# The third burst of k^T v one q group earlier, and a small first transfer from W_qkv

## The chip, the cores and the metric

The kernel runs on one core of a Trainium2 chip. The time is the device time of one execution in microseconds (us), as the median of several runs. TensorE (PE) multiplies matrices and has its own queue of weight loads (PEld); VectorE (DVE), ScalarE (ACT) and GpSimd (POOL) work on tiles; SyncE (SP) issues most transfers. Every engine runs its own instructions in order, and engines wait for each other through semaphores. Beside the queues that move data, the trace has queues of the kind "instruction": packets that bring the engines' programs.

## The reference, cut to what matters

The sizes are S = 2048 tokens, D = 640, 32 heads of 20, and F = 1536. All inputs are bf16.

```python
h  = x + A(_layernorm(x), A_wqkv, A_w_phi, A_wo)
h2 = h + B(_layernorm(h), B_w_gate, B_w_up, B_w_down)

def A(x, wqkv, w_phi, wo):          # linear attention
    q, k, v = split_heads(x @ wqkv)
    pq, pk  = q @ w_phi, k @ w_phi  # per head, 20 x 20
    phi_q = concat(softmax(pq), softmax(-pq))
    phi_k = concat(softmax(pk), softmax(-pk))
    kv, z = phi_k^T @ v, sum over tokens of phi_k
    return merge_heads((phi_q @ kv) / (phi_q @ z + 1e-6)) @ wo

def B(x, w_gate, w_up, w_down):
    return (gelu(x @ w_gate) * (x @ w_up)) @ w_down
```

## The kernel before

The 2048 tokens are 16 tiles of 128, in four groups `b` of four. The order of the instructions of TensorE and SyncE is written out by hand; what the other engines do is written in the same order.

At the start SyncE issues the tiles of x (`x_sb`) and the v part of W_qkv (`Wv`, in three pieces, lines 194 to 197), and ScalarE issues `wphi` (line 191) and loads its table of functions (line 192). TensorE runs 30 matmuls on ones (`warm`, line 230), then transposes the first two tiles of x (`tr_c`) and computes the v of tiles 0 and 1 from the first pieces of `Wv` (`v_part`, line 312). `BD` (line 433), which VectorE builds from `wphi`, is needed by `fold`, which multiplies W_phi into the k and q parts of W_qkv (`Wk2`, `Wq2`).

The loop of line 494 goes over the 16 token tiles `t`. `k_tile(t)` multiplies the normalised tile by `Wk2` (10 matmuls) and ScalarE exponentiates it with both signs into `Ek[t]` (line 340). `k_norm(t)` sums each head on VectorE (line 347), takes the reciprocal (line 351) and multiplies it into `Ek[t]` (line 355): the second sign on GpSimd always, the first on GpSimd for the tiles of `VP` (9, 11, 12 and 13 among them), on VectorE for the others.

`kv_tile(t)` (line 374) adds phi_k^T v of tile t into one PSUM tile `kvp`: 32 heads, each one weight load of 32 columns and one matmul over 40 columns. So a tile is 32 pairs of very short instructions. They are not run tile by tile but in bursts: tiles 0 to 3 at t = 9 and tiles 4 to 8 at t = 13 (`KVG`), tiles 9 to 12 at t = 15 (`KVQ`, the third burst), and tiles 13 to 15 after the loop (line 540).

At t = 15 the loop of line 508 also computes the first four of the 13 q groups. `q_mm(j)` (line 396) has 10 matmuls over 512 columns for a group of two, 5 for a group of one; `q_exp(j)` (line 401) exponentiates the group on ScalarE with both signs. `QG` lists the groups: group 0 reads the token group b = 1, group 1 reads b = 0. `KVQ` says behind which q group the third burst stands:

```python
for j in range(len(QT)):
    if t == QT[j]:
        q_mm(j)
        q_exp(j)
        for i in KVQ.get(j, ()):
            kv_tile(i)
```

At t = 13 SyncE is given the load of `Wo` (800 KB, line 534), and after the loop those of `Wg` (line 538), `Wu` (line 554) and `Wd` (line 559). The `Wg` load is held back by a small copy on GpSimd (line 536) that reads the exponentials of q group 2. After `kv_mask` the kernel runs the rest of the q groups mixed with the attention of the first tiles (`attn_a` and so on), and then the feed-forward part (`gate_up`, `down`) with the attention of later tiles woven in.

Of the kernel before, what the change touches and what calls it, by code (L numbers as in the profile page):

```python
# [8 lines left out]
BF16 = mybir.dt.bfloat16  # L9
# [8 lines left out]
def kernel(  # L18
# [12 lines left out]
    nc = tc.nc  # L31
    P = 128
    S = 2048
    D = 640
# [19 lines left out]
    T3 = 3  # L54

    KVG = {9: (0, 1, 2, 3), 13: (4, 5, 6, 7, 8)}
    KVQ = {1: (9, 10, 11, 12)}
    VC = Dh + 1
    KC = Dh + 2

# [17 lines left out]
    const = ctx.enter_context(tc.tile_pool(name="const", bufs=1))  # L78
# [20 lines left out]
    BD = const.tile([P, NC, 8, Dh], BF16, name="BD")  # L99
    nhalf = const.tile([P, 2], F32, name="nhalf")  # L100
    eps = const.tile([P, 1], F32, name="eps")

    def eq(t, c, s):
        for E, g in zip(Eq, QG):
            if t // 4 * NC + c in g:
                return E[:, g.index(t // 4 * NC + c), s, t % 4 * P:(t % 4 + 1) * P]
# [81 lines left out]
    nc.gpsimd.memset(eps, EPS)  # L188
    nc.sync.dma_start(x_sb[0][:, 0:1, :], x_v[:, 0:1, :])
    nc.sync.dma_start(x_sb[0][:, 1:2, :], x_v[:, 1:2, :])  # L190
    nc.scalar.dma_start(wphi, phi_v.rearrange("(c p) f -> p c f", p=P))
    nc.scalar.add_instruction(mybir.InstLoadActFuncSet(name=nc.get_next_instruction_name(), act_func_set_id=6))
    nc.sync.dma_start(x_sb[0][:, 2:3, :], x_v[:, 2:3, :])  # L193
# [174 lines left out]
    def kv_tile(t):  # L368

        E = Ek[t].rearrange("p s (h f) -> p s h f", f=Dh)  # L370
        for i in range(QH):
            for r in range(4):
                h = r * QH + i
                nc.tensor.matmul(kvp[QUAD[r], :, i * Dh:(i + 1) * Dh], lhsT=vF[t % NV][:, h * VC:h * VC + 32],  # L374
                                 rhs=E[:, :, h, :], start=(i == t == 0), stop=(t == NT - 1), skip_group_check=True)
# [23 lines left out]
    def q_exp(j, signs=(0, 1)):  # L399
        for s in signs:  # L400
            nc.scalar.activation(Eq[j][:, :, s, :], pqs[j][:, 0:len(QG[j])], ACTF.Exp, scale=(1.0, -1.0)[s])  # L401
# [92 lines left out]
    for t in range(NT):  # L494
# [13 lines left out]
# [6 lines that stand above are left out]
# [423 lines left out]
```

## Time and profile before

| | |
|---|---|
| median of 3 runs | 271.94 us (271.78 to 272.07) |
| the profiled execution | 272.4 us |
| its span, first to last instruction | 270.7 us |
| PE busy | 265.7 us, 98% of the span, 2867 matmuls and 2867 weight loads |
| DVE / ACT / POOL busy | 174.9 / 138.9 / 101.2 us |
| granted TensorE clock, mean | 0.999 |
| instruction packets of queue q8 | 22, together 0.36 MB |

The profile is of one execution. Its page gives busy time by engine, the chain of work that ended last, the costliest groups of instructions, and the transfers. The trace behind it answers by time: the chain in order of time, all instructions of a stretch, the transfers of a stretch by queue, or the busy time and the granted clock of each engine in a stretch. "issue" in a row means that the engine was idle and the trace shows no wait that ended then. A matmul's end is modelled, its start is not.

### The profile page before, as it was taken

Reading aid. Unit: us, or ns where it says so; the run is one execution under the profiler, and the core shown is the slowest. Engines: PE = TensorE matmul, PEld = TensorE weight load, DVE = VectorE, ACT = ScalarE, POOL = GpSimd, SP = SyncE. Lnnn points to the kernel's source line nnn. Section 1 sums busy time; section 2 is a strip of 40 time slices with the busy share of each in tenths; the row PEclk is TensorE's granted clock in tenths of the full one; section 3 lists DMA queues with packets and bytes.
Section 4 is the critical chain, followed back from the end, with each engine's and each line's share of the span. In section 5 each row is a group of like instructions: output and inputs, shape, how many; then the busy total and the mean of one; then the engine's idle time right before and its main releaser. Section 6 shows DMA issues by size and latency. Waiting matters only on the chain.

```text
span 270.7 us, 7046 instructions
## 1 busy us (share of the span) xinstructions
PE 265.7 (98%) x2867; PEld 171.3 (63%) x2867; DVE 174.9 (65%) x347; ACT 138.9 (51%) x249; POOL 101.2 (37%) x238
## 2 busy tenths in 40 slices
PE   7999999999999999999999999999999999999995
PEld 6777777755455877788755455775555476444574
DVE  5889999996877767876466783568673332333322
ACT  5789998876789675245541356421544300322100
POOL 5548988796002335376211564014661100000000
PEclk9999999999999999999999999999999999999999
DMA  6998257250678432442201222102222101000011
GB/s 187 225 199 169 54 99 110 38 150 2 234 246 244 155 101 56 41 104 51 52 24 51 48 50 51 48 3 75 77 44 52 24 24 51 24 0 0 4 48 48
DMA packets 45264, 22.10 MB, mean 82 GB/s; under 512 B 37808, under 2 KB 43184, under 8 KB 45232
## 3 DMA queue, kind: packets, MB, share of 16 engines
q1 hardware_dynamic: 44576, 21.64, 32.6%
q8 instruction: 22, 0.36, 0.6%
q10 hardware_dynamic: 656, 0.03, 0.2%
q14 instruction: 10, 0.08, 0.1%
HBM read 10.18 MB, written 2.62 MB: 47 GB/s over the span
## 4 chain that ended last, share of the span: by engine, by line
PE 96%; DMA 2%; SPq 0%; issue 0%; DVE 0%
PE gu L767 39%; PE pd L789 19%; PE pq L396 8%; PE pk L296 8%; PE po L707 8%; PE pv L296 7%; PE kvp L374 2%; PE pv L312 2%; DMA Wv<-in_A_wqkv_dram 2%; PE ab L618 1%; PE wa L248 1%; PE ab L585 1%; PE tp L164 0%; SPq L193 0%; SPq L190 0%
## 5 line engine op out<-in xcount | busy, mean ns | idle before, releaser
L770 ACT ACTIVATE g<-gu 128x512 bf16<-128x512 f32 (+1 forms) x60 | 30.4, 510 | 73.8 <-PE gu L767 72.9
L773 DVE TENSOR_TENSOR GT<-gu,g 128x512 bf16<-128x512 f32 (+1 forms) x60 | 34.4, 580 | 46.7 <-PE gu L767 38.8
L767 PE MATMUL gu<-LN2T,Wg 128*128 128x512 bf16 (+1 forms) x300 | 61.8, 337 | 0.0
L767 PE MATMUL gu<-LN2T,Wu 128*128 128x512 bf16 (+1 forms) x300 | 61.7, 336 | 0.0
L789 PE MATMUL pd<-Wd,GT 128*128 128x320 bf16 (+4 forms) x396 | 53.9, 295 | 0.0
L789 PEld LDWEIGHTS <-GT 128*128 128x128 bf16 x396 | 37.6, 98 | 14.5 <-DVE GT L773 0.2
L767 PEld LDWEIGHTS <-Wu 128*128 128x128 bf16 x300 | 29.4, 98 | 22.6
L767 PEld LDWEIGHTS <-Wg 128*128 128x128 bf16 x300 | 29.0, 98 | 21.2
L296 PEld LDWEIGHTS <-LN1T 128*128 128x128 bf16 x290 | 27.9, 98 | 10.5
L355 POOL TENSOR_TENSOR E<-E,rs 128x640 bf16<-128x640 bf16 x25 | 31.6, 1299 | 4.4 <-DVE rs L351 4.1
L791 DVE TENSOR_TENSOR y<-pd,x_sb 128x320 bf16<-128x320 f32 (+4 forms) x33 | 15.8, 480 | 24.2 <-PE pd L789 24.2
L707 PE MATMUL po<-Wo,oT 128*128 128x320 bf16 x160 | 24.5, 299 | 0.0
L296 PE MATMUL pk<-Wk,LN1T 128*128 128x320 bf16 x160 | 24.4, 299 | 0.0
L396 PE MATMUL pq<-LN1T,Wq 128*128 128x512 bf16 x100 | 22.9, 379 | 0.0
L347 DVE TENSOR_REDUCE sk<-E 128x64 f32<-128x1280 bf16 x16 | 22.9, 1430 | 0.0
L401 ACT ACTIVATE Eq<-pq 128x1024 bf16<-128x1024 f32 (+1 forms) x26 | 19.9, 831 | 3.5 <-PE pq L396 3.3
L340 ACT ACTIVATE E<-pk 128x640 bf16<-128x640 f32 x28 | 18.7, 746 | 3.0 <-PE pk L296 3.0
L707 PEld LDWEIGHTS <-oT 128*128 128x128 bf16 x160 | 15.6, 98 | 7.3 <-ACT oT L165 0.2
L296 PE MATMUL pv<-Wv,LN1T 128*128 128x320 bf16 x130 | 19.8, 299 | 0.0
L151 ACT ACTIVATE ln<-x_sb,v,rstd 128x640 bf16<-128x640 bf16 x14 | 12.9, 920 | 13.4 <-POOL v L746 13.2
L396 PEld LDWEIGHTS <-Wq 128*128 128x128 bf16 x100 | 9.4, 98 | 10.3
L682 DVE TENSOR_TENSOR tt<-AB,w 128x1280 bf16<-128x1280 f32 x10 | 15.1, 1506 | 0.4 <-POOL w L675 0.3
(120 smaller groups left out, 290.6 us busy)
## 6 DMA issues: line engine op xcount, KB each, us to landing
out_dram<-y SPq DMA_DIRECT2D x15, 160.0 KB, 1.8
x_sb<-in_A_x_dram SPq DMA_DIRECT2D x6, 320.0 KB, 4.0
Wu<-in_B_w_up_dram SPq DMA_DIRECT2D x1, 1920.0 KB, 8.9
Wg<-in_B_w_gate_dram SPq DMA_DIRECT2D x2, 768.0 KB, 5.8
Wd<-in_B_w_down_dram SPq DMA_DIRECT2D x1, 1440.0 KB
Wo<-in_A_wo_dram SPq DMA_DIRECT2D x1, 800.0 KB, 5.2
x_sb<-in_A_x_dram SPq DMA_DIRECT2D x4, 160.0 KB, 3.3
Wv<-in_A_wqkv_dram SPq DMA_DIRECT2D x2, 320.0 KB, 4.2
```

Source lines behind the costliest of these rows:

```text
L296: nc.tensor.matmul(ps[:, u, 0:HD], lhsT=lnT(t, c), rhs=W[:, c, u * HD:(u + 1) * HD], start=(c == 0), stop=(c == NC - 1))
L340: nc.scalar.activation(Ek[t][:, s, :].rearrange("p (u f) -> p u f", u=2), pk[:, :, 0:HD], ACTF.Exp, scale=((lnp[t][2], nrstd[t]) if t in C ...
L347: nc.vector.reduce_sum(sk, Ek[t].rearrange("p s (h f) -> p (s h) f", f=Dh), axis=AX.X)
L355: eng.tensor_tensor(e, e, rs[:, s * H:(s + 1) * H, None].to_broadcast([P, H, Dh]), ALU.mult)
L396: nc.tensor.matmul(pqs[j][:, i, :], lhsT=Wq2[:, kc, c * P:(c + 1) * P], rhs=LN1T[b][:, kc, :], start=(kc == 0), stop=(kc == NC - 1))
L401: nc.scalar.activation(Eq[j][:, :, s, :], pqs[j][:, 0:len(QG[j])], ACTF.Exp, scale=(1.0, -1.0)[s])
L707: nc.tensor.matmul(pos[u], lhsT=st[t][:, c, :], rhs=Wo[:, c, u * HD:(u + 1) * HD], start=(c == 0), stop=(c == NC - 1))
L767: nc.tensor.matmul(gu[i][:, 0:n], lhsT=W[:, c, f * P:(f + 1) * P], rhs=LN2T[b][:, c, a0:a1], start=(c == 0), stop=(c == NC - 1))
L770: nc.scalar.activation(g[:, 0:n], gu[0][:, 0:n], ACTF.Gelu_apprx_tanh)
L773: nc.vector.tensor_tensor(st[b, "g", f][:, a0:a1], gu[1][:, 0:n], g[:, 0:n], ALU.mult)
L789: nc.tensor.matmul(pd[:, 0:f1 - f0], lhsT=st[b, "g", f][:, tl * P:(tl + 1) * P], rhs=Wd[:, f, f0:f1], start=(f == 0), stop=(f == NF - 1), ...
L791: nc.vector.tensor_tensor(y[:, f0:f1], pd[:, 0:f1 - f0], x_sb[b][:, tl, f0:f1], ALU.add)
```

## The change

The third burst, `kv_tile` of tiles 9 to 12, moves from behind q group 1 to behind q group 0. And a new transfer is put first in ScalarE's queue, ahead of `wphi`: 16 bf16 values (32 bytes) of every fifth row of W_qkv, from the first columns of the v part, into a tile `ahead` that nothing reads. It has 128 pieces, one for each partition, and touches rows 0, 5, 10 and so on to 635. Every other instruction stays as it was, and the counts of TensorE's instructions too.

```diff
@@ -54,7 +54,7 @@
     KVG = {9: (0, 1, 2, 3), 13: (4, 5, 6, 7, 8)}
-    KVQ = {1: (9, 10, 11, 12)}
+    KVQ = {0: (9, 10, 11, 12)}
@@ -99,6 +99,7 @@
     eps = const.tile([P, 1], F32, name="eps")
+    ahead = const.tile([P, 16], BF16, name="ahead")
@@ -188,6 +189,7 @@
     nc.sync.dma_start(x_sb[0][:, 0:1, :], x_v[:, 0:1, :])
     nc.sync.dma_start(x_sb[0][:, 1:2, :], x_v[:, 1:2, :])
+    nc.scalar.dma_start(ahead, A_wqkv.rearrange("(p r) n -> p r n", p=P)[:, 0, 2 * D:2 * D + 16])
     nc.scalar.dma_start(wphi, phi_v.rearrange("(c p) f -> p c f", p=P))
```

## The prediction

> **What bounds the kernel now.** I read the page's busy table first, then the chain of work that ended last, then the chain in order of time around the moved burst, then the transfers of that stretch, and last the first 7 us.
>
> ```profile
> PE 265.7 (98%) x2867; PEld 171.3 (63%) x2867; DVE 174.9 (65%) x347; ACT 138.9 (51%) x249; POOL 101.2 (37%) x238
> PE 96%; DMA 2%; SPq 0%; issue 0%; DVE 0%
> q8 instruction: 22, 0.36, 0.6%
> ```
>
> TensorE is busy for 98% of the span and makes 96% of the chain. After 6.45 us its chain has one hole before the end. So whatever delays or saves TensorE time in the middle reaches the end nearly in full. The chain in order of time (start, length, what) has that hole inside the third burst:
>
> ```profile
> 57.20 4.32 PE pq L396 x20
> 61.52 0.97 PE kvp L374 x109
> 62.50 0.48 issue
> 62.98 0.30 PE kvp L374 x19
> 63.28 3.34 PE pq L396 x15
> 66.62 0.87 PE kvp L374 x96
> ```
>
> The burst stops after 109 of its 128 pairs, in the middle of tile 12, before an instruction that carries no wait; the hole is 0.48 us and "issue" names no releaser. I take it for a lack of instructions. The queue q8 moves 22 packets of 16 KB, and TensorE has 2 x 2867 = 5734 instructions: one packet for 261 of them, near 256 of 64 bytes. A burst uses them at two in 8.9 ns (0.97 us / 109). The transfers in two neighbouring stretches, first 56.1 to 60.6 us, then 60.6 to 62.9 us:
>
> ```profile
> DMA packets 1306, 0.97 MB, mean 215 GB/s; under 512 B 677, under 2 KB 1306, under 8 KB 1306
> q1 hardware_dynamic: 1306, 0.97, 80.2%
> Wo<-in_A_wo_dram SPq DMA_DIRECT2D x1, 800.0 KB, 5.2
> ...
> q8 instruction: 1, 0.02, 2.8%
> q1 hardware_dynamic: 17, 0.01, 1.8%
> ```
>
> In the first stretch only data moves: a transpose, then `Wo`, issued at 56.17 us. In the second comes one instruction packet, which by the trace starts at 60.64 us, as the last packet of `Wo` ends (60.69 us), and takes 1.04 us, to 61.68 us. TensorE goes on at 62.98 us, 1.30 us later. The next packet starts at 64.10 us, 1.12 us after it went on, as if entering a block asks for the one after it. The packet at 72.59 us likewise starts only when the load of `Wg` ends (72.69 us). So I read: a block is asked for when the one before it is entered, it stands in line behind the data already queued, and is usable 1.3 us after it lands.
>
> **Part 1, the burst.** Nothing is added or removed: 128 pairs change places with 10 matmuls of q group 1. What counts is where the block border falls. TensorE's instructions are equal in number, so the border is the same instruction number in both orders. Before the hole stand 20 instructions of group 0, 21 of group 1 (one is a wait) and 218 of the burst, 259; the block of 256 thus begins with the fourth instruction of group 0. With the burst directly behind group 0, the 256 are 17 of group 0 and 239 of the burst: the border comes after 119 pairs, with 9 left.
>
> Times in the new order: group 0 begins at 57.20 us as before and takes half of 4.32, 2.16 us, to 59.36 us. The burst's data is there: the eight GpSimd products from 54.45 to 64.90 us are two each for tiles 11, 12 and 13 and one each for 14 and 15, 1.27 us each, so that tile 12's second, the fourth, ends at 59.40 us, while the burst comes to tile 12 only 96 x 8.9 ns = 0.85 us after 59.36. Tiles 9 to 11 are done by 57 us. The border is reached at 59.36 + 119 x 8.9 ns = 60.42 us. The block's packet depends on `Wo`, which SyncE issues behind transposes of work that stands ahead of group 0, so nothing before 59.36 us changes, and it is usable at 62.98 us again. The hole becomes 62.98 - 60.42 = 2.56 us. Then come 9 pairs (0.14 us, from 0.30 for 19) to 63.12 us and group 1, 2.16 us, to 65.28 us. In the trace of before, group 2 starts at 63.28 us: 2.00 us earlier. The change in short lets TensorE stand idle while group 1, which used to run in that time, is still to do.
>
> Is any of it given back? Behind the burst TensorE has no idle time that could take it up: the chain is TensorE without a hole to 267.83 us. Nor is more lost: group 3 needs the PSUM tile of group 0, whose exponentials end at 61.34 us as before. The exponentials of group 1 (1.94 us) run from 65.3 to 67.3 us, before group 2 ends at 67.44 us, so those of group 2, the copy on POOL that releases `Wg` on SP's queue, and everything behind them shift by the same 2.0 us. The next block's packet was asked for on entering this one, at 62.98 us, and is usable at 64.10 + 0.93 + 1.30 = 66.3 us as before; its border, near 67.3 us, comes at 69.3 us. No hole there. Cost of part 1: +2.00 us.
>
> The idle time itself is a risk for the clock. The nearest row is the end of the kernel: busy time by engine (us, with the count of instructions), granted clock, share of DMA and GB/s in three stretches.
>
> ```profile
> 262.00:266.90 4.90, 4.90 (x42) 3.76 (x41) 1.48 (x3) 0.00 (x0) 0.00 (x0) 1.00 0.19 67
> 266.90:270.30 3.40, 0.92 (x16) 0.74 (x13) 0.65 (x2) 0.00 (x0) 0.00 (x0) 1.00 0.18 48
> 270.30:270.70 0.40, 0.00 (x0) 0.00 (x0) 0.00 (x0) 0.00 (x0) 0.00 (x0) 0.52 0.00 0
> ```
>
> There the clock fell to about half after 3.4 us with 0.92 us of work. 3.4 us around the new hole would hold at least 0.84 us of work, and mostly more, as the hole would have to lie wholly in one such stretch.
>
> **Part 2, the transfer.** ScalarE issues it in about the 0.47 us that `wphi`'s issue takes at 0.79 us; `wphi` and the table load (1.28 us, ending at 2.56) move back by 0.47 us. Cover: ScalarE waits for x until 4.09 us, 1.06 us after the new end of the table load; `wphi` lands 2.9 us after its issue, so near 4.2 us, and is first read at 6.64 us. With those covers gone each would cost up to 0.47 us. On the 16 DMA engines, shared with x and `Wv`, 128 packets of 32 bytes cost what `wphi`'s 640 of 40 bytes do each, 11 ns: 0.09 us an engine.
>
> The first matmuls on `Wv` show what could be gained:
>
> ```profile
> 2.18 4.22 DMA Wv<-in_A_wqkv_dram
> 5.46 1.29 ACT L165 COPY LN1T<-tp 128x640 bf16<-128x640 bf16 x2
> 6.20 0.10 PEld L312 LDWEIGHTS <-LN1T 128*128 128x128 bf16 x1 [0.30 <-ACT LN1T L165]
> 6.45 1.79 PE L312 MATMUL pv<-Wv,LN1T 128*128 128x320 bf16 x12 [0.37 <-DMA Wv<-in_A_wqkv_dram]
> 2.00:3.50 1.50, 1.50 (x17) 1.50 (x16) 0.54 (x6) 0.57 (x1) 1.23 (x9) 1.00 0.98 240
> 3.50:4.50 1.00, 1.00 (x13) 0.86 (x10) 0.95 (x3) 0.41 (x1) 0.65 (x13) 1.00 0.75 119
> 4.50:7.00 2.50, 1.71 (x20) 1.28 (x20) 2.14 (x6) 2.33 (x7) 0.52 (x2) 1.00 0.98 336
> ```
>
> Around 3.5 to 4.5 us, when the queue comes to `Wv`, the rate dips to 119 GB/s between 240 and 336, with packets of up to 0.98 us in the trace: some 0.6 us lost, and perhaps a first touch of W_qkv's memory, which the new transfer would take earlier. Even so TensorE can't start on `Wv` before its weights, loaded from 6.20 us: gain at most 6.45 - 6.26 = 0.19 us. The other end: the same 0.6 us is lost in front of x's first tile instead, whose landing (VectorE starts on it at 3.36 us) leads to that weight load; 6.26 + 0.6 is 0.4 us later than now. The row nearest is the wait of 0.37 us on `Wv` itself, so I take a small gain, -0.1 us, and keep -0.2 and +0.4.
>
> **Sum.** +2.00 - 0.10 = +1.9 us. The profiled execution took 272.4 us, 1.7 around its span of 270.7 us, and lies 0.5 us above the median of the runs, 271.94. Its own forecast is 274.3; that of the median, which I give, 273.8 us, 0.7% slower.
>
> **Rivals.** (a) The packet gets through while `Wo` moves. It must start by 60.42 - 1.30 - 1.04 = 58.1 us, and then the hole is gone, old and new: 271.94 - 0.48 - 0.1 = 271.4 us, faster. Each us later costs one, up to the 2.56. For it: block and request stand there from about 57.3 us on. Against it: with the old order the same request waited until 60.64. The Trainium skill, "DMA: Bandwidth & Descriptors" (Queues, rings and completion order), says that each DMA engine goes round-robin between the queues that have work, which would favour this rival; the starts at 60.64 and 72.59 us, each as the data ended, disagree. "Runtime: NRT & Kernel Launch" (Instruction fetch mechanics) of the same skill even gives TensorE room for 2048 instructions and calls the fetch mostly hidden; a hole of 0.48 us with no wait at a 256-instruction border speaks against it here.
> (b) The hole has nothing to do with a block and goes with the burst, 0.48 us wherever it stands: 271.94 - 0.1 = 271.8 us, no change.
> (c) The clock halves for one stretch of 3.4 us after the hole, which loses 1.7 us: 275.5 us. For it the row at 266.9 us; against it that 0.84 us is the least and not the usual work of such a stretch. The skill's "TensorE: Matmul & The Clock Gate" (Part 1: The HAM clock gate) asks for about one idle window of 3.4 us, and by that rule nothing would be lost.
>
> **How the numbers follow.** Forecast, hole of about 2.6 us: 0.66, itself 273.3 to 274.4 by the bounds of part 2 and some 0.3 us for where the border falls. (c) 0.11. (a) 0.10 and a packet partly ahead, between 271.6 and 273.3, 0.06. (b) 0.07. From 272.8 to 275.6 lie the forecast, (c) and some of the partial case, about 0.8. What a measurement of this kernel can tell from no change is about 0.2%, 0.54 us. Faster: (a) less a little, 0.10; same: (b) and a little, 0.09; slower: 0.81.
>
> **What would show it.** In the chain, an "issue" row of 2.3 to 2.8 us inside the third burst, behind about 119 pairs, ending near 63 us; an instruction packet that starts with the end of `Wo`; group 2 starting near 65.2 us; the first matmul on `Wv` between 6.2 and 6.9 us; granted clock at 1.00 from 62 to 70 us. A hole ending early, or none, proves the reading of the packet queue wrong; a start on `Wv` outside those bounds, part 2.

## The result, and the profile after

The changed kernel takes 273.39 us (median of 8 runs, 272.26 to 277.14), the kernel before 271.98 us (271.78 to 272.87, 8 runs). The ratio is 1.0046, with a 95% interval of 1.0029 to 1.0063: slower by about half a per cent, where 0.7% was forecast. All ratios here leave out runs of over 1.5% above the fastest of the same kernel (here one, 277.14 us); medians and ranges keep them. The profiled execution took 273.48 us, with a span of 271.8 us. But its trace is not the one that was forecast.

The busy table and the chain that ended last, from the page of the changed kernel:

```profile
PE 265.3 (98%) x2867; PEld 170.9 (63%) x2867; DVE 175.1 (64%) x347; ACT 138.9 (51%) x249; POOL 100.5 (37%) x238
PE 93%; DMA 3%; DVE 1%; SPq 0%; issue 0%
```

TensorE still bounds the kernel, with transfers for 3% of the chain instead of 2%. The chain in order of time (start, length, what), first at the start, then around the burst, then where a new wait has come in:

```profile
2.18 5.00 DMA Wv<-in_A_wqkv_dram
7.22 1.79 PE pv L314 x12
...
58.09 2.16 PE pq L398 x10
60.24 1.13 PE kvp L376 x128
61.38 5.50 PE pq L398 x25
...
83.19 4.20 DMA LN2T<-ln
87.39 0.14 issue
87.52 3.44 PE gu L769 x30
```

The first matmul on `Wv` starts at 7.22 us, 0.77 later than before (6.45). The burst runs through in 1.13 us without any hole. And at 87.4 us TensorE waits for a transposed tile, which it did not before. The waits of TensorE (in us: total, times, longest) say the same:

```profile
PE pv L314 <- DMA Wv<-in_A_wqkv_dram: 1.5, 1, 1.5
PE gu L769 <- DMA LN2T<-ln: 0.9, 1, 0.9
```

Where the 1.1 us of span went, by the starts of the same work in both traces: +0.77 at the first matmul on `Wv` (7.22 against 6.45) and +0.89 at q group 0 (58.09 against 57.20); +0.26 at group 2 (61.38 + 2.16 = 63.54 against 63.28), so the burst without its hole gave back 0.63; +1.22 at the first matmul of `gate_up` (87.52 against 86.30), most of it the 0.9 us wait. That wait is for a transpose behind the load of `Wu`, which took 10.1 us from issue to landing in this execution and 8.9 before.

The transfers from 56.1 to 60.6 us, the stretch that held only data before:

```profile
q1 hardware_dynamic: 1097, 0.71, 61.8%
q8 instruction: 1, 0.02, 2.1%
Wo<-in_A_wo_dram SPq DMA_DIRECT2D x1, 800.0 KB, 5.8
```

The instruction packet is now inside it. By the trace it starts at 58.23 us, when the first packet of `Wo` starts (58.24), and not when the last one ends.

### The profile page after: what moved, and what is told of

Read it like the earlier page. It is cut to its first block, busy times and chain, and to the rows that moved or that the text cites. A ratio compares the mean times of both kernels' runs of the same rounds, so it can differ in the third digit from the quotient of the medians.

```text
span 271.8 us, 7047 instructions
## 1 busy us (share of the span) xinstructions
PE 265.3 (98%) x2867; PEld 170.9 (63%) x2867; DVE 175.1 (64%) x347; ACT 138.9 (51%) x249; POOL 100.5 (37%) x238
## 4 chain that ended last, share of the span: by engine, by line
PE 93%; DMA 3%; DVE 1%; SPq 0%; issue 0%
PE gu L769 38%; PE pd L791 19%; PE pk L298 8%; PE po L709 8%; PE pv L298 7%; PE pq L398 6%; DMA Wv<-in_A_wqkv_dram 2%; PE kvp L376 2%; PE pv L314 2%; DMA LN2T<-ln 2%; PE ab L620 1%; PE wa L250 1%; PE ab L587 1%; DVE x_sb L718 1%; DVE stats L122 1%; PE tp L165 0%
## 5 line engine op out<-in xcount | busy, mean ns | idle before, releaser
L122 DVE BATCH_NORM_STATS2 stats<-x_sb 128x6 f32<-128x320 bf16 x32 | 13.9, 475 | 2.0 <-DMA x_sb<-in_A_x_dram 2.0
## 6 DMA issues: line engine op xcount, KB each, us to landing
Wu<-in_B_w_up_dram SPq DMA_DIRECT2D x1, 1920.0 KB, 10.1
```

The lines of the kernel that those rows point to most:

```text
L122: nc.vector.bn_stats(stats[:, j, i, :], xt[:, i * HD:(i + 1) * HD])
```

## The experiments

Each ratio is against the kernel before, run beside it on the same chip. "Hole" is TensorE's idle time at the block border, of the one profiled execution. The theories are: (A) the hole is the wait for an instruction packet that races with `Wo`'s data; (B) it goes with the burst for some other reason; and for the transfer (C) and (D), where its cost comes from.

### The burst alone

```diff
-    KVQ = {1: (9, 10, 11, 12)}
+    KVQ = {0: (9, 10, 11, 12)}
```

> The burst behind group 0, without the new transfer. Theory A (a block of 256 TensorE instructions is fetched when the one before it is entered, and the fetch queues behind Wo's data if it comes second): the request and Wo's first packet come within some 0.3 us of each other, so single runs fall on two values: no hole, 272.0 - 0.5 = 271.5 us, or a hole of 2.0 to 2.6 us, 273.5 to 274.0 us. Theory B (the 0.48 us hole goes with the burst and has no block behind it): 272.0 us in all runs, hole 0.48 us.

Measured: 272.99 us (12 runs, 272.08 to 277.17) against 272.12; 1.0045 (1.0016 to 1.0074). Seven runs lie between 272.08 and 273.09, five between 274.38 and 277.17, none between. The profiled one, 272.61 us, is of the first group:

```profile
59.73 1.06 PE kvp L374 x119
60.79 0.33 issue
61.12 0.23 PE kvp L374 x9
...
61.73 5.13 PE pq L396 x23
```

The hole stands behind 119 pairs with 9 left, exactly where the block border was worked out, but is 0.33 us long. The packet starts at 57.67 us, just ahead of `Wo`'s first (57.77), and takes 1.97 us, while `Wo`'s packets move. Two groups of runs speak for (A), though the upper one lies above the 273.5 to 274.0 us expected. The lower group was expected 0.5 us under the kernel before; by its median (272.57) it is 0.45 us above, which these runs do not explain.

The same kernel once more:

> The kernel with the burst behind group 0 alone once more, for a second profile and a few more times. Theory A (race of the packet with Wo's data): the profile shows one of two pictures, the packet starting before or with Wo's first data and a hole under 0.4 us, or the packet starting with the end of Wo's data and a hole of 2.0 to 2.6 us; single times near 272.5 us or over 274.3 us, and few between.

Measured: 276.97 and 278.15 us; 1.020 (1.017 to 1.023, two runs only). This profile holds the other picture. The chain in order of time:

```profile
59.82 1.06 PE kvp L374 x119
60.88 2.93 issue
63.81 0.23 PE kvp L374 x9
64.04 0.32 PE pq L396
64.36 0.14 issue
64.50 6.73 PE pq L396 x23
```

The transfers of the same execution, first 56.1 to 60.6 us, then 60.6 to 62.9 us:

```profile
q1 hardware_dynamic: 1201, 0.84, 69.0%
...
q1 hardware_dynamic: 127, 0.14, 17.0%
q8 instruction: 1, 0.02, 2.6%
```

Again 119 pairs, then 2.93 us of nothing, somewhat more than the 2.0 to 2.6 expected. The packet starts at 61.45 us, when `Wo`'s data ends (61.44), and lands at 62.42; TensorE goes on 1.39 us later. The busy time of each engine, the granted clock, the share of DMA and GB/s in four stretches:

```profile
57.00:61.00 4.00, 3.83 (x133) 2.26 (x133) 3.79 (x5) 3.30 (x6) 4.00 (x4) 1.00 0.74 218
61.00:64.00 3.00, 0.19 (x10) 0.15 (x10) 2.90 (x3) 0.80 (x1) 3.00 (x4) 1.00 0.04 12
64.00:68.00 4.00, 3.87 (x18) 1.49 (x12) 2.01 (x2) 0.00 (x0) 1.33 (x1) 0.57 0.02 4
68.00:72.00 4.00, 4.00 (x111) 2.11 (x109) 0.00 (x0) 3.75 (x4) 0.00 (x0) 1.00 0.00 0
```

After 3 us with 0.19 us of work the clock is at 0.57 in the mean of the next 4 us. With the stretches cut where the clock changes, it is 0.50 from 64.32 to 67.73 us, and in the 3.41 us before that TensorE worked 0.51 us. The hole costs 2.6 us more than the one of the first profile and the clock 1.6 (the same 23 matmuls take 6.73 us, against 5.13): together 4.2 of the 4.36 us between the two executions. This is the forecast hole, and rival (c) on top of it.

### Wo out of the way, and in the way

```diff
         if t == 10:
+            nc.sync.dma_start(Wo, wo_v)
             transpose_to(LN1T[0][:, :, P:2 * P], ln_a(1), False)
...
-        if t == 13:
-            nc.sync.dma_start(Wo, wo_v)
```

With the burst behind group 0:

> The burst behind group 0, and the load of Wo issued at t = 10, when the transfers have been idle for some us, so that no large transfer is in front of the instruction packet asked for near 57 us. Theory A (the packet races with Wo's data): the packet starts near 58.2 us, takes 0.9 to 1.0 us, the hole is under 0.3 us in the profile, and the slow group of runs over 274 us (5 of 12 with the burst alone) is gone; median 0.4 to 0.5 us under the kernel before. Theory B (the slow runs have another cause than Wo): 4 to 6 of 12 runs still over 274 us.

Measured: 272.36 us (11 runs, 271.57 to 272.94) against 272.25; 0.9998 (0.9983 to 1.0013). No run over 274 us. The packet starts at 58.06 us, `Wo` is long over (48.2 to 53.1 us), and the burst has no hole:

```profile
57.41 2.16 PE pq L396 x10
59.57 1.14 PE kvp L374 x128
60.71 5.50 PE pq L396 x25
```

(A) holds for the upper group of times, and (B) falls: nothing else about the burst was changed, and that group is gone. The expected gain of 0.4 to 0.5 us under the kernel before did not come.

With the burst behind group 1:

> The burst behind group 1 as before, Wo issued at t = 10. Theory A: no hole in the burst, 0.5 us under the kernel before, and equal to the kernel with the moved burst and the early Wo within 0.3 us. Theory B: the hole of 0.48 us stays, no change.

Measured: 271.91 us (11 runs, 271.59 to 272.89) against 272.25; 0.9987 (0.9969 to 1.0004). No hole (the burst takes 1.13 us). The median is 0.34 us under the kernel before, with an interval that reaches no change, and 0.45 us under the kernel with the moved burst and the early `Wo`, where 0.3 at most was expected; both kernels' runs go from about 271.6 to 272.9 us. The same kernel once more, as the version that might beat both:

> The kernel before with Wo issued at t = 10, once more with more rounds, as the version that could beat both: the hole of 0.48 us goes and nothing else changes, 0.3 to 0.5 us under the kernel before.

Measured: 272.03 us against 272.11; 0.9997 (0.9987 to 1.0007). The hole is gone again, the time can't be told from the kernel before. A reason may be that the kernel before does not always have the hole: the three kernels with its order of the burst and a new transfer (below) show none. In one of them the packet starts at 57.73 us, ahead of `Wo`'s first at 57.81. In the other two it starts 2.3 and 2.0 us behind the start of group 0, in the middle of `Wo`'s data: at 60.49 us with `Wo` from 58.41 to 63.54, and at 62.18 us with `Wo` from 60.35 to 65.05.

`Wo` issued by ScalarE, earlier:

```diff
             ln_ap(0, on_act=True)
+            nc.scalar.dma_start(Wo, wo_v)
...
-        if t == 13:
-            nc.sync.dma_start(Wo, wo_v)
```

> The burst behind group 0, with Wo issued by ScalarE right behind the normalisation of tile 0, some 1 us earlier than SyncE does, so that its data is always in the queues before the packet is asked for. Theory A: the packet starts only when Wo's data ends, 59.5 to 60.6 us, the hole is 1.5 to 2.6 us in all runs, median 1.0 to 2.2 us over the kernel before. Theory B: no hole over 0.5 us, time as with the burst alone.

Measured: 273.12 us (11 runs, 272.17 to 274.55) against 272.25; 1.0025 (1.0006 to 1.0044). The hole is 0.84 us, again behind 119 pairs:

```profile
60.21 1.06 PE kvp L374 x119
61.27 0.84 issue
62.11 0.23 PE kvp L374 x9
```

Theory A expected a hole of 1.5 to 2.6 us and a median 1.0 to 2.2 us over the kernel before; the hole is 0.84 us and the median 0.87 over, so (A) misses both, and (B), which expected no hole over 0.5 us, falls. `Wo`'s data runs from 54.47 us, earlier than I had reckoned, and ends at 59.29. The end of the hole follows the packet again, but the packet starts at 59.76 us, 0.47 us behind the end of `Wo`: the small packets of a transpose move until then, and what it waited for was not tried apart. This profile is of the slowest of the 11 runs (274.55 us).

### The block border moved

42 TensorE instructions less at the start, in about the same time, put every border 42 instructions later in the program.

```diff
-    warm(*[512] * 2, *[P] * 28)
+    warm(*[512] * 9)
```

> The kernel before with 7 warm-up matmuls of 512 columns in the place of 28 of 128 (42 instructions less in the same time), so that every block border of TensorE's program comes 42 instructions later. Theory A: the block's request moves from group 0 into the first pairs of the burst (about 61.4 us), it is usable 3.5 us later, near 64.9 us, and the border falls on the second or third matmul of group 2: a hole of about 2 us there instead of 0.48 in the burst, 1.2 us slower, 273.2 us. Theory B: hole of 0.48 us in the burst as before, 272.0 us.

Measured: 273.14 us (12 runs, 272.43 to 274.91) against 272.12; 1.0033 (1.0011 to 1.0054). The chain:

```profile
61.58 1.13 PE kvp L374 x127
62.72 0.32 PE pq L396
63.04 0.35 issue
63.39 2.76 PE pq L396 x12
```

The burst runs through, and the hole has gone to the start of group 2, where the border now is; some 0.05 us of idle time stands there in other profiles too. That it stays at a count of instructions, and not with the burst, is (A). Its size is not: 0.35 us instead of 2, so that the expected time of 273.2 us was met by something else. The packet started at 61.01 us, as `Wo`'s data ended (61.01 us), so it had been asked for before TensorE reached the burst at 61.58; I had it asked for only there.

> The burst behind group 0, no new transfer, 42 instructions less at the start. Theory A: the request comes in the first pairs of the burst, about 59.5 us, the packet starts when Wo's data ends (60.7 us) and is usable at 63.0 us; the border falls on the start of group 2, reached near 63.0 us: no hole or under 0.3 us, 271.5 us, so that here the moved burst is the faster order by 1.7 us against the kernel with the burst behind group 1 and the same 42 less. Theory B: 272.0 us, no difference to that kernel.

Measured: 272.94 us (12 runs, 272.41 to 274.05) against 272.12; 1.0033 (1.0016 to 1.0051). No hole, as (A) said, with the packet at 62.08 us as `Wo`'s data ended (62.08), but not faster: the turn of 1.7 us between the two orders, which I expected, is 0.2 us. Both kernels are some 0.9 us slower than the kernel before, and their profiles (272.43 and 273.06 us) do not name one cause: the second waited for a tile of x that took 5.26 us to land, the first had no such wait. So these two show the place of the border, and nothing about times.

### The new transfer alone

The burst behind group 1, with the two lines of `ahead` as in the change.

> The new transfer, with the burst behind group 1 as before. Theory A (the transfer itself slows what follows it in the DMA engines, as the profile after shows): first matmul on Wv at about 7.2 us instead of 6.45, time 272.0 + 0.8 = 272.8 us. Theory B (the late Wv of that one profile was chance): first matmul on Wv at 6.3 to 6.5 us and 271.8 to 272.0 us.

Measured: 272.78 us (12 runs, 272.05 to 275.40) against 272.12; 1.0043 (1.0017 to 1.0069). The first matmul on `Wv` starts at 7.24 us: (A). Four of the 12 runs lie between 273.93 and 275.40 us, and three of these have a mean clock of 0.994, like the profiled run of the next kernel, whose trace shows where that comes from.

Another tensor:

```diff
-    nc.scalar.dma_start(ahead, A_wqkv.rearrange("(p r) n -> p r n", p=P)[:, 0, 2 * D:2 * D + 16])
+    nc.scalar.dma_start(ahead, B_w_gate.rearrange("(p r) n -> p r n", p=P)[:, 0, 0:16])
```

> The burst behind group 1 as before; the new transfer reads 32 bytes of every fifth row of W_gate instead of W_qkv, all else the same. Theory C (the cost lies in reading W_qkv itself early, at the rows that the v load reads next): first matmul on Wv near 6.5 us as before, 272.0 to 272.3 us. Theory D (any such transfer, or wphi being pushed back, costs it): first matmul on Wv near 7.2 us, 272.6 to 272.9 us.

Measured: 273.01 us (11 runs, 272.11 to 275.03) against 272.25; 1.0043 (1.0020 to 1.0067). The first matmul on `Wv` starts at 7.89 us, so the cost is not in W_qkv's addresses: (D). This profile also has a low clock. Its chain in order of time:

```profile
2.18 5.67 DMA Wv<-in_A_wqkv_dram
7.89 2.84 PE pv L314 x12
```

Its busy times by stretch (columns as above):

```profile
4.30:7.90 3.60, 1.58 (x20) 1.23 (x19) 3.08 (x8) 3.22 (x10) 0.52 (x2) 1.00 0.98 327
7.90:11.00 3.10, 3.10 (x17) 1.99 (x17) 0.49 (x1) 0.05 (x1) 2.38 (x9) 0.59 1.31 166
```

After a wait of 2.0 us for `Wv` the clock falls to about 0.6 in the mean of that stretch, and the same 12 matmuls take 2.84 us instead of 1.79. With the stretches cut where the clock changes, it is 0.50 from 8.47 to 11.88 us, and in the 3.41 us before that TensorE worked 1.41 us. The mean clock of this run is 0.994.

The same transfer, second in ScalarE's queue:

```diff
     nc.scalar.dma_start(wphi, phi_v.rearrange("(c p) f -> p c f", p=P))
+    nc.scalar.dma_start(ahead, A_wqkv.rearrange("(p r) n -> p r n", p=P)[:, 0, 2 * D:2 * D + 16])
```

> The burst behind group 1 as before; the new transfer comes second in ScalarE's queue, behind wphi. Theory D1 (the cost comes from wphi being pushed back onto the v load): first matmul on Wv near 6.5 us, 272.1 to 272.4 us. Theory D2 (any transfer of 128 small pieces beside the x and v loads leaves some of the 16 DMA engines behind): near 7.2 us, 272.6 to 273.0 us.

Measured: 272.29 us (11 runs, 271.93 to 273.48) against 272.11; 1.0013 (1.0000 to 1.0027). The first matmul on `Wv` starts at 6.63 us. So most of the cost comes from the transfer standing ahead of `wphi`, as D1 has it; what in that place makes it was not separated. The four profiles with it in front have x early and one end of `Wv` late: the second tile of x lands at 3.73 us in the changed kernel, 4.07 before, but of the 16 engines that carry the first piece of `Wv` twelve are done by 6.23 us and the last four at 6.77 to 7.18; before, all were done between 5.07 and 6.40. Why a few engines fall behind when `wphi`'s 640 small packets come later (up to 3.57 us instead of 3.17) was not tried apart, for example by pushing `wphi` back with no transfer in front.

### The changed kernel once more

> The changed kernel once more. If its time is the sum of its two parts, the first matmul on Wv stands at 7.0 to 7.4 us in this profile too, and the runs are those of the burst alone (some near 272.5, some over 274.3 us) moved up by 0.7 us: most at 272.8 to 273.8 us, some at 275 us and more.

Measured: 273.70 us (12 runs, 272.03 to 280.43) against 272.11; 1.0049 (1.0026 to 1.0071). Eight runs from 272.03 to 273.77, four from 275.78 to 280.43. Profiled at 273.68 us: the first matmul on `Wv` at 7.56 us and a hole of 0.40 us behind 119 pairs, with the packet at 58.91 and `Wo`'s first at 58.86 us. The packet comes just behind `Wo`'s first here, and still was not held until the end of `Wo`. The first matmul on `Wv` is later than the 7.0 to 7.4 us expected, and the slowest run, with a mean clock of 0.982, longer than anything the parts had shown. The medians of the parts add up: 0.87 us for the burst alone and 0.66 for the transfer alone, 1.53 together, against 1.59 here and 1.41 in the first runs.

## Why the prediction was right or wrong

The number was right: 273.8 forecast, 273.39 measured, slower. Most of the reason was not, and that the two agree is luck.

**The bound and the border, right.** TensorE is still the chain, and the block border is real: with the burst behind group 0 the hole came behind 119 pairs in all four profiles that have one there, and moved with the program when 42 instructions were taken out.

**The size of the hole, wrong as a certainty.** The step that failed is "the block's packet depends on `Wo` [...] and it is usable at 62.98 us again". I took one execution's order of arrival for a rule. In four profiles the packet starts within 0.1 us of `Wo`'s first packet (58.23 and 58.24; 57.67 and 57.77; 57.73 and 57.81; 58.91 and 58.86), and there the hole is 0 to 0.4 us; in the one with the burst alone where it came 3.6 us behind that packet, the hole was 2.93 us (forecast: 2.56). The forecast put 0.66 on the second picture and 0.10 on the first, rival (a). With the burst alone 7 of 14 runs lie over 274 us, so about even would have been the better split. The +2.00 us of part 1 is thus 0.45 us in the median of the lower runs and 2.3 to 6.0 in the others, three of which have a lowered mean clock too (0.994, 0.994 and 0.988). Of the 20 runs of the changed kernel, those over 274 us can't be put down to the hole alone, since the transfer alone has runs with a lowered clock as well.

**The queueing, half right.** The rule that a packet waits for the end of the data ahead of it had two examples, and one is misread. At 72.59 us the load of `Wg` was not ending. The transfers from 72.5 to 74 us:

```profile
q1 hardware_dynamic: 129, 0.35, 59.8%
q8 instruction: 1, 0.02, 4.0%
```

The last packet of the two transfers of `Wg` under way there ends at 74.89 us. In the other example `Wo`'s last packet ends at 60.92 us, not at 60.69. A packet that comes behind the start of the load does wait: until 60.64 us in the profile before and 61.45 in the burst alone, near the end of `Wo`. But with the new transfer alone, and with the one from W_gate, it waits until 60.49 and 62.18 us only and starts in the middle of `Wo`. What it waits for is open. The round-robin of the Trainium skill's "DMA: Bandwidth & Descriptors" (Queues, rings and completion order) fits the packets that start beside `Wo` and then take 1.36 to 2.12 us instead of 0.9 to 1.1, but not the two in the middle of `Wo`, which take 0.97 and 0.93. Whether it can make waits of 2 to 4 us depends on how much an engine takes from one queue before it turns to the next, which no run here shows.

**The transfer, wrong in sign and beyond my bound.** I took -0.1 us, with ends at -0.2 and +0.4. It costs +0.77 us in this profile and 0.66 by the medians with the transfer alone. I had counted its own packets and a loss moved in front of x; x did come earlier. The cost shows where the transfer stands ahead of `wphi`, a shift that I had costed at nothing because it was covered: the reader of `wphi` was covered, but the v load was not, and its slowest engines end later. How the one makes the other is open. Nor had I counted that a longer wait on `Wv` can lower the clock: with the transfer alone 3 of 12 runs, and with the one from W_gate 3 of 11, have the mean clock of 0.994 that the profiled one shows behind that wait.

**Nothing given back, nothing more lost: mostly right.** The burst's 0.63 us passed through to the rest. The 0.9 us wait for `LN2T` in the changed kernel stands behind a slower `Wu` load. It came in one other profile (the one with `Wo` on ScalarE) and in none of the others, the second one of the changed kernel among them, so nothing here ties it to the change; its cause is open.

**Rival (c), the clock, came true** in a place where I looked and in one where I did not: 0.57 after the hole of 2.93 us, 0.59 after a wait of 2.0 us for `Wv`. By the rule that the prediction cites from the Trainium skill's "TensorE: Matmul & The Clock Gate" (Part 1: The HAM clock gate), an idle window of about 3.4 us, neither would have happened; here 0.51 and 1.41 us of work in the 3.41 us before did not keep the clock up.

**Rival (b) falls** by the profiles without a hole.

So the forecast time was reached by another sum: in the medians +0.66 us for the transfer where -0.1 was forecast, and +0.87 for the burst where +2.00 was; the second is a mix of runs with a small hole, with the forecast hole, and with the lowered clock.

## What to carry to other kernels

When two requests meet in the profile, look at how far apart they start before you call the order a rule; at 0.1 us apart either may come first, and the forecast is two times with two chances. A second example for a rule is worth one more look at the trace. A burst of very short matmuls needs its instruction packet to be in before it comes to the block border, so keep large loads away from the time when the packet is fetched; with the burst moved that took away the times over 274 us, with the order of before it brought no gain clear of the noise. A transfer that is cheap in itself can cost by what it pushes back in its queue, and the loads that share the engines are to be checked, not only the reader of the pushed tile.

## What the runs showed of the hardware

- TensorE's program comes in blocks of 256 instructions, each used up to the last: the hole stands at the same count in five profiles, and with 42 instructions less at the start it moved out of the burst to the start of group 2. From the end of the packet to the next instruction it took 1.25 to 1.48 us in the six holes seen.
- This instruction packet of 16 KB takes 0.9 to 1.1 us with no load of `Wo` beside it, 1.36 to 2.12 in the four profiles where it starts with the load, and 0.97 and 0.93 in the two where it starts in the load's middle. Behind the start of the load it waits: near to the load's end in two profiles (60.64 and 61.45 us), into its middle in two others (60.49 and 62.18).
- The clock falls to half for 3.41 us after waits of 2.0 and 2.93 us, with 1.41 and 0.51 us of work in the 3.41 us before; it stayed at 1.00 after waits of 1.5 and 1.6 us in the two profiles of the changed kernel.
- In the four profiles with the small transfer in front, two to four of the 16 engines ended the first piece of `Wv` late, the last of them at 7.18 to 7.85 us, 0.9 to 1.6 after the bulk. In the ten others the last ended at 6.32 to 7.01 us; the 7.01 is of the kernel before with `Wo` early, and with the transfer in second place it was 6.59.
